# A chunked recurrence with top-k routing on one core: scores and comparisons read PSUM, the one-hot table in six operations, fetched rows turned a step later, VectorE's order changed

## The chip, the cores and the metric

The kernel runs on one core of a Trainium2 chip. The metric is device time in microseconds (us) of one execution; the median of three runs is given. Engines are named as in the profile: PE (TensorE matmuls), DVE (VectorE), ACT (ScalarE), POOL (GpSimd) and SP, whose queue issues nearly all transfers.

## The reference, cut to what matters

Two blocks follow each other. The first is a linear recurrence over 768 tokens for 4 batches and 8 heads of 48 channels, with a decay `w` and a bonus `u`; the second scores each of the 768 rows of a batch, takes the 128 best, and sends those alone through a two-layer network of width 1024.

```
for t:  y[t] = r[t] @ (state + u*k[t] (x) v[t]);  state = w*state + k[t] (x) v[t]
x = y as (batch, 768, 384)
scores = x @ w_gate                      # one number per row
top = the 128 rows of the batch with the highest scores
out = x;  out[top] = x[top] + sigmoid(scores[top]) * (relu(x[top] @ w1) @ w2)
```

## The kernel before, in words

**Tiling.** A unit is 128 tokens of one batch with all 8 heads; there are 24 units, 6 to a batch (NC = 6). The loop over `n` (line 515) does one unit per step. In a step, `inner(n)` (PE) forms the state update and the products of keys and queries in the PSUM tile `rp`; `added(n, 0)` and `added(n, 1)` (DVE, line 264) add the running state and give `g`, and ACT scales `g` by the decay into the next state `z` (line 267, four pieces for each); `masked(n)` (DVE, line 259) puts the products into the matrix `at`; `turn(n+1)` (PE) transposes the next unit's keys and queries into `pk` and `pr`, ACT copies `pk` (line 231), and `turned` (DVE, line 236) scales `pr`; `bonus_sum(n+1)` (DVE, line 208) sums the bonus products that POOL made; POOL scales keys (`scaled`), builds the diagonal of `at` from the sums (`diagonal`, line 212) and makes the next bonus products (`bonus`). Then `outer(n-1, n)` on PE completes the output `y` of unit n-1 and begins that of unit n. Last, `rows_of_x(n-1)` copies `y` from PSUM to the SBUF tile `x` on ACT (line 321) and `finish(n-1)` multiplies `x` by the gate weights on DVE, summing to the scores `sc` (line 326), and stores `x` through SP's queue.

**Routing.** `scores_along(b, j)` has PE turn the 128 scores of unit j into rows of a PSUM tile and ACT copy them to `srow` (line 344). `compare(b, j)` on DVE compares them with the scores of units 0 to j, one operation each (line 351), and once for ties (line 353). After the sixth unit `count` adds up the counts, `rank` gives every row its rank, `match` (DVE, line 378) builds the one-hot table `oh` of 128 ranks by 768 rows in one operation, `pick` turns it into row numbers, `fetch` (POOL) gathers those rows from DRAM by an indirect transfer into `xr`, and `chosen` has PE transpose them (line 411). The network follows in eight parts, four `hidden` (line 431) and four `expert` (line 443); `leave` (DVE, line 451) adds the result and POOL scatters it.

**Order.** Every engine and every queue works in the order in which the code is written; the semaphores follow from the data. `plan(b)` (lines 479 to 494) puts the routing of batch b into later steps, in one of two places: "turn" (before `outer`) or "end" (after `finish`). With n = 6(b+1): unit j is compared at the end of step n-4+j, ranked at the end of step n+2, matched at the turn of n+3, fetched at its end, and `chosen` stands at the end of n+4; the eight parts lie two to a step in steps n+5 to n+8. What is left for the last batches is written out after the loop (lines 553 to 586), the parts of batch 2 that remain filling PE while batch 3 is ranked.

**Buffers.** The PSUM name `m` has two banks, and all of the routing and the network share them. `y` has two. Loads run four units ahead; SP's queue has, step by step, the three loads of unit n+4, a slice of the weights in steps 5 to 11, and the store of unit n-1.

## Time and profile before

| | us |
|---|---|
| median of 3 runs | 198.11 (195.6 to 199.34) |
| profiled execution, its own time | 198.54 |
| its span, first to last instruction | 196.8 |
| PE busy | 159.7 (81%) |
| DVE busy | 126.2 (64%) |
| POOL busy | 114.8 (58%) |
| ACT busy | 79.5 (40%) |
| moved by DMA | 24.52 MB |

The busy times are of the whole span; the loop over the 24 units runs from about 13 to 167.5 us, and what follows is the ranking and the network of the last batch. A step of the loop is read here from the start of its first `g` (line 264) to the start of the next step's. In a trace, idle time carries the engine whose event ended it.

### The profile page before, as it was taken

Reading aid. Unit: us, or ns where it says so; the run is one execution under the profiler, and the core shown is the slowest. Engines: PE = TensorE matmul, PEld = TensorE weight load, DVE = VectorE, ACT = ScalarE, POOL = GpSimd, SP = SyncE. Lnnn points to the kernel's source line nnn. Section 1 sums busy time; section 2 is a strip of 40 time slices with the busy share of each in tenths; the row PEclk is TensorE's granted clock in tenths of the full one; section 3 lists DMA queues with packets and bytes.
Section 4 is the critical chain, followed back from the end, with each engine's and each line's share of the span. In section 5 each row is a group of like instructions: output and inputs, shape, how many; then the busy total and the mean of one; then the engine's idle time right before and its main releaser. Section 6 shows DMA issues by size and latency. Waiting matters only on the chain.

```text
span 196.8 us, 8480 instructions
## 1 busy us (share of the span) xinstructions
PE 159.7 (81%) x3608; PEld 136.5 (69%) x3608; DVE 126.2 (64%) x435; ACT 79.5 (40%) x267; POOL 114.8 (58%) x131
## 2 busy tenths in 40 slices
PE   1579967757569947999999299999997789996980
PEld 1269956556559936999678299997686689855840
DVE  3835788888897784287688967776889734821000
ACT  2135755425635362365554255365245633300200
POOL 4499999795568785538439957755569600022002
PEclk9999999999975795899999759999999769999999
DMA  6999997789896699087357817554312111102001
GB/s 108 198 179 179 199 198 175 150 218 190 209 229 169 124 260 224 3 213 155 74 127 163 201 44 161 127 120 88 83 42 85 43 40 45 43 7 73 0 0 40
DMA packets 81508, 24.52 MB, mean 125 GB/s; under 512 B 76352, under 2 KB 80704, under 8 KB 81472
## 3 DMA queue, kind: packets, MB, share of 16 engines
q1 hardware_dynamic: 79856, 22.03, 51.4%
q0 software_dynamic: 512, 1.57, 2.6%
q10 hardware_dynamic: 1104, 0.40, 1.4%
q8 instruction: 28, 0.46, 1.0%
q14 instruction: 8, 0.07, 0.1%
HBM read 18.48 MB, written 5.51 MB: 122 GB/s over the span
## 4 chain that ended last, share of the span: by engine, by line
PE 38%; DVE 17%; issue 15%; ACT 11%; POOL 9%; DMA 7%; POOLq 1%; DVEq 0%
PE m L431 8%; PE y L298 6%; DMA xr<-out_dram,idx 6%; ACT z L267 6%; DVE scr L326 5%; DVE gt L351 5%; PE pk L221 4%; PE rp L254 4%; PE pr L224 3%; PE rp L246 3%; PE y L310 3%; PE y L289 3%; DVE scr L353 3%; ACT x L321 3%; POOL at L212 2%
## 5 line engine op out<-in xcount | busy, mean ns | idle before, releaser
L267 ACT ACTIVATE z<-g,wp 128x48 f32<-128x48 f32 x176 | 44.5, 323 | 58.8 <-DVE g L264 58.8
L212 POOL TENSOR_TENSOR at<-dia,du 128x512 f32<-128x512 f32 x24 | 26.6, 1109 | 36.1 <-DVE du L208 36.1
L298 PE MATMUL y<-vin,at 64*64 64x48 f32 x768 | 39.5, 232 | 9.0 <-DVE g L264 8.7
L298 PEld LDWEIGHTS y<-vin,at 64*64 64x64 f32 x768 | 33.4, 146 | 14.9 <-DVE g L264 11.3
L326 DVE SCALAR_TENSOR_TENSOR scr<-x,wg 128x384 f32<-128x384 f32 x24 | 22.3, 929 | 24.7 <-ACT x L321 24.6
L310 PE MATMUL y<-z,rh 48*64 48x48 f32 x352 | 28.7, 229 | 0.0
L204 POOL TENSOR_TENSOR rku<-rk,ub 128x384 f32<-128x384 f32 x24 | 25.9, 1080 | 1.9
L202 POOL TENSOR_TENSOR rk<-rpad,kin 128x384 f32<-128x384 f32 x23 | 26.8, 1167 | 0.0
L431 PE MATMUL m<-xt,w 128*128 128x128 f32 x192 | 25.9, 290 | 0.6 <-ACT xt L413 0.6
L431 PEld LDWEIGHTS m<-xt,w 128*128 128x128 f32 x192 | 24.1, 203 | 1.3 <-ACT xt L413 0.8
L351 DVE TENSOR_SCALAR_CACHE_REDUCE gt<-srow,sc 128x128 bf16<-128x128 f32 x84 | 24.0, 336 | 0.7 <-ACT srow L344 0.7
L198 POOL TENSOR_TENSOR kw<-kin,wk 128x384 f32<-128x384 f32 x23 | 23.7, 1031 | 0.1
L264 DVE TENSOR_TENSOR g<-rp,z 128x192 f32<-128x192 f32 x40 | 14.1, 353 | 15.0 <-ACT z L267 8.7
L443 PE MATMUL m<-w,ht 128*128 128x384 f32 x64 | 23.1, 497 | 0.1
L310 PEld LDWEIGHTS y<-z,rh 48*64 48x64 f32 x352 | 20.8, 146 | 0.0
L289 PE MATMUL y<-z,rh 48*64 48x48 f32 x352 | 20.7, 240 | 0.0
L254 PE MATMUL rp<-rh,kh 48*64 48x64 f32 x768 | 19.6, 244 | 1.0 <-issue 0.6
L221 PE MATMUL pk<-ident,kw 128*112 128x128 f32 x92 | 17.6, 322 | 0.8 <-POOL kw L198 0.8
L224 PE MATMUL pr<-ident,rpad 128*112 128x128 f32 x96 | 17.7, 314 | 0.6 <-issue 0.5
L254 PEld LDWEIGHTS rp<-rh,kh 48*64 48x64 f32 x768 | 16.7, 156 | 1.4 <-issue 1.4
L246 PE MATMUL rp<-vin,kw 64*48 64x48 f32 x704 | 16.1, 225 | 1.9 <-POOL kw L198 1.9
L259 DVE COPY_PREDICATED at<-mask,rp 128x512 f32<-128x512 uint32 x24 | 17.4, 723 | 0.0
(86 smaller groups left out, 238.2 us busy)
## 6 DMA issues: line engine op xcount, KB each, us to landing
rpad<-in_r_dram SPq DMA_DIRECT2D x24, 192.0 KB, 5.0
vin<-in_v_dram SPq DMA_DIRECT2D x24, 192.0 KB, 3.2
out_dram<-x SPq DMA_DIRECT2D x24, 192.0 KB, 3.2
kin<-in_k_dram SPq DMA_DIRECT2D x23, 192.0 KB, 4.6
w<-in_moe_w_dram SPq DMA_DIRECT2D x3, 512.0 KB, 5.0
w<-in_moe_w_dram SPq DMA_DIRECT2D x4, 384.0 KB, 4.4
k<-in_k_dram SPq DMA_DIRECT2D x1, 192.0 KB
ub<-in_u_dram ACTq DMA_DIRECT2D x1, 192.0 KB, 4.6
```

Source lines behind the costliest of these rows:

```text
L202: nc.gpsimd.tensor_mul(rk, rpads[n % NIN][:, :, :D], KIN[n])
L204: nc.gpsimd.tensor_mul(RKU[n], rk, ub)
L212: nc.gpsimd.tensor_mul(AT[n], dia[:, None, :].to_broadcast([128, H, C]), DU[n].rearrange("t i p -> t (i p)")[:, :, None].to_broadcast([128 ...
L221: nc.tensor.transpose(pk[:CH, hp, :], two_heads(kws[n % 3] if keys is None else keys, hp), ident)
L254: nc.tensor.matmul(out=rp[ts, i, hp * C : (hp + 1) * C], lhsT=KH[n][rows, hp, ts], rhs=RH[n][rows, hp, ts], start=True, stop=True)
L267: nc.scalar.activation(to[:, hp, :], g[:, hp, :], AF.Copy, scale=wc[:, hp : hp + 1])
L289: nc.tensor.matmul(out=YP[m][ts, 2 * hp + i, :], lhsT=RH[m][rows, hp, ts], rhs=z[rows, hp, :], start=(hp == 0), stop=False, skip_group_che ...
L298: mm = nc.tensor.matmul(out=y[ts, 2 * hp + i, :], lhsT=AT[n][ts, i * NP + hp, :], rhs=VIN[n][ts, 2 * hp + i, :], start=False, stop=False, ...
L310: nc.tensor.matmul(out=y[ts, 2 * hp + c, :], lhsT=RH[n][rows, hp, ts], rhs=z[rows, hp, :], start=False, stop=(hp == NP - 1), skip_group_ch ...
L326: nc.vector.scalar_tensor_tensor(scr, x, 1.0, wg, op0=OP.mult, op1=OP.mult, accum_out=sc[b][:, c : c + 1])
L351: nc.vector.tensor_scalar(GT[b][:, c, j, :], SR[b, j], sc[b][:, c : c + 1], None, op0=OP.is_gt, op1=OP.add, accum_out=counts[b % 2][:, c, ...
L431: nc.tensor.matmul(out=ph[:, f % 4, :], lhsT=w1[:, d, f * 128 : (f + 1) * 128], rhs=XT[b, z][:, d, :], start=(d == 0), stop=(d == KD - 1))
```

## The change

Six edits. `finish` reads `y` in PSUM for the scores, and the copy to `x` on ACT is made to wait for that. `scores_along` leaves the turned scores in PSUM, and `compare` reads them there; ACT's copy to `srow` is gone. `match` uses six operations, one for each unit, each also writing an accumulator that nobody reads (`found`), on a table of 128 columns in place of 768; the offset of each unit goes into a new column of `counts`. `compare` and `count` move from the end of a step to its turn. `chosen` moves from the end of step n+4 to the turn of n+5, and the eight parts move half a step back: one at the end of n+5, two in each of n+6 to n+8, one at the turn of n+9. `bonus_sum(n+1)` moves ahead of `added(n, 1)`.

```diff
--- before.py
+++ after.py
@@ -171,15 +171,19 @@
     ones = const.tile([128, 2], BF16)
     nc.vector.memset(ones[:, 0:1], -1.0)
     nc.vector.memset(ones[:, 1:2], 0.0)
-    counts = [const.tile([128, NC, NC + 1], F32, name=f"counts{i}") for i in range(2)]
+    counts = [const.tile([128, NC, NC + 2], F32, name=f"counts{i}") for i in range(2)]
     for x in counts:
         nc.vector.memset(x, 0.0)
-    slots = const.tile([128, NC, 128], F32)
+    slots = const.tile([128, 128], F32)
+    found = const.tile([128, NC], F32)
     tok = const.tile([128, NU, 2], BF16)
 
     def late_tables():
-        nc.gpsimd.iota(slots, pattern=[[-128, NC], [1, 128]], base=0, channel_multiplier=0,
+        nc.gpsimd.iota(slots, pattern=[[1, 128]], base=0, channel_multiplier=0,
                        allow_small_or_imprecise_dtypes=True)
+        for x in counts:
+            nc.gpsimd.iota(x[:, :, NC + 1], pattern=[[128, NC]], base=0, channel_multiplier=0,
+                           allow_small_or_imprecise_dtypes=True)
         nc.gpsimd.iota(tok[:, :, 0], pattern=[[0, NU]], base=0, channel_multiplier=1,
                        allow_small_or_imprecise_dtypes=True)
         nc.gpsimd.iota(tok[:, :, 1], pattern=[[T, NU]], base=0, channel_multiplier=0,
@@ -316,21 +320,21 @@
 
     stores, moves = {}, {}
 
-    def rows_of_x(n):
-        b, c = divmod(n, NC)
-        return nc.scalar.copy(xa[b][:, c, :], YP[n].rearrange("t h d -> t (h d)"))
-
     def finish(n):
         b, c = divmod(n, NC)
+        y = YP[n].rearrange("t h d -> t (h d)")
         x = xa[b][:, c, :]
-        nc.vector.scalar_tensor_tensor(scr, x, 1.0, wg, op0=OP.mult, op1=OP.mult,
-                                       accum_out=sc[b][:, c : c + 1])
+        score = nc.vector.scalar_tensor_tensor(scr, y, 1.0, wg, op0=OP.mult, op1=OP.mult,
+                                               accum_out=sc[b][:, c : c + 1])
+        left = nc.scalar.copy(x, y)
+        tc.add_manual_dep(left.ins, score.ins.name, wait_for, reason="one reader of y's bank at a time")
         st = nc.sync.dma_start(out=out[b, c * T : (c + 1) * T, :], in_=x)
         for (bb, _), others in moves.items():
             if bb != b:
                 for o in others:
                     tc.declare_no_dep(st.ins, o.ins, reason="rows of another batch")
         stores.setdefault(b, []).append(st)
+        return left
 
 
     SR, GT, QQ, XR, XT, IDX, GA, HT, PH, PE, OH = ({} for _ in range(11))
@@ -339,9 +343,8 @@
 
     def scores_along(b, j):
         p = psum.tile([128, 512], F32, name="m", bufs=2)
-        nc.tensor.transpose(p[:, :128], sc[b][:, j : j + 1].to_broadcast([128, 128]), ident)
-        SR[b, j] = work.tile([128, 128], F32, name="srow", bufs=3)
-        nc.scalar.copy(SR[b, j], p[:, :128])
+        SR[b, j] = p[:, :128]
+        nc.tensor.transpose(SR[b, j], sc[b][:, j : j + 1].to_broadcast([128, 128]), ident)
 
     def compare(b, j):
 
@@ -370,12 +373,13 @@
 
     def match(b, z):
         oh = OH[b, z] = work.tile([128, NC, 128], BF16, name="oh")
+        q = QQ[b]
         if z:
             q = work.tile([128, NC], F32, name="qz")
             nc.vector.tensor_scalar(q, QQ[b], float(-128 * z), None, op0=OP.add)
-        else:
-            q = QQ[b]
-        nc.vector.tensor_tensor(oh, slots, q[:, :, None].to_broadcast([128, NC, 128]), op=OP.is_equal)
+        for c in range(NC):
+            nc.vector.tensor_scalar(oh[:, c, :], slots, q[:, c : c + 1], None, op0=OP.is_equal, op1=OP.add,
+                                    accum_out=found[:, c : c + 1])
 
     def pick(b, z):
         p = psum.tile([128, 512], F32, name="m", bufs=2)
@@ -480,18 +484,18 @@
         n = (b + 1) * NC
         for j in range(NC):
             step(n - NC + j + 2, "turn", scores_along, b, j)
-            step(n - NC + j + 2, "end", compare, b, j)
-        step(n + 1, "end", count, b)
+            step(n - NC + j + 2, "turn", compare, b, j)
+        step(n + 1, "turn", count, b)
         step(n + 2, "end", rank, b)
         for z in range(NST):
             step(n + 3, "turn", match, b, z)
             step(n + 3, "end", pick, b, z)
             step(n + 3, "end", fetch, b, z)
-            step(n + 4, "end", chosen, b, z)
+            step(n + 5, "turn", chosen, b, z)
         parts = [p for z in range(NST) for p in mlp(b, z)]
         per = -(-len(parts) // 8)
         for i, (f, a) in enumerate(parts):
-            step(n + 5 + i // per // 2, ("turn", "end")[i // per % 2], f, *a)
+            step(n + 5 + (i // per + 1) // 2, ("end", "turn")[i // per % 2], f, *a)
 
     for b in range(B):
         plan(b)
@@ -531,11 +535,12 @@
         masked(n)
         if n + 1 < NU:
             pr = turn(n + 1)
+        if n + 1 < NU:
+            bonus_sum(n + 1)
         if c < NC - 1:
             added(n, 1)
         if n + 1 < NU:
             turned(n + 1, pr)
-            bonus_sum(n + 1)
         if n + 2 < NU:
             scaled(n + 2)
         if n + 1 < NU:
@@ -545,8 +550,7 @@
         work_at(n, "turn")
         outer(n - 1 if n else None, n, G[n, 0])
         if n:
-            left = rows_of_x(n - 1)
-            finish(n - 1)
+            left = finish(n - 1)
         work_at(n, "end")
 
 
@@ -565,7 +569,6 @@
     scores_along(last, NC - 2)
     outer(NU - 1, None, left)
     compare(last, NC - 2)
-    rows_of_x(NU - 1)
     finish(NU - 1)
     some(NST)
     scores_along(last, NC - 1)
```

## Rows read from the trace of the kernel before

**Rows 1.** Busy time of each engine by stage, one row per window of time.

```profile
core 0: us, PE busy (x) PEld busy (x) DVE busy (x) ACT busy (x) POOL busy (x), PEclk, DMA share, GB/s
...
21.88:56.79 34.91, 24.40 (x813) 20.98 (x811) 29.45 (x98) 16.96 (x62) 28.95 (x30) 0.99 0.87 194
56.79:69.37 12.58, 12.06 (x296) 11.12 (x296) 9.40 (x27) 6.15 (x22) 8.81 (x9) 0.61 0.72 163
69.37:77.66 8.29, 4.27 (x116) 3.70 (x117) 4.55 (x17) 3.45 (x12) 6.42 (x6) 0.75 1.09 271
77.66:105.91 28.25, 28.25 (x636) 24.27 (x637) 19.88 (x71) 13.98 (x44) 15.06 (x15) 0.95 0.53 117
105.91:114.14 8.23, 4.69 (x145) 4.26 (x144) 7.66 (x17) 2.97 (x11) 7.21 (x9) 0.81 0.76 166
...
120.57:146.72 26.15, 26.15 (x630) 22.16 (x629) 19.80 (x72) 12.57 (x43) 16.21 (x16) 1.00 0.47 105
...
152.81:160.19 7.38, 5.46 (x122) 4.72 (x120) 4.05 (x18) 3.55 (x12) 3.10 (x5) 0.73 0.19 56
...
167.50:196.80 29.30, 21.92 (x142) 16.33 (x142) 6.11 (x30) 3.29 (x8) 3.15 (x5) 0.99 0.08 27
```

**Rows 2.** Chain of work that ended last, step 3: start, length, what.

```profile
29.08 0.97 ACT z L267 x4
30.05 0.15 ACT srow L344
30.20 0.38 ACT x L321
...
30.60 1.06 DVE scr L326 x2
31.67 0.54 DVE gt L351 x4
32.20 0.47 DVE scr L353 x2
```

**Rows 3.** DVE in order of time, step 4: start, length, line, operation.

```profile
32.60 0.35 DVE L264 TENSOR_TENSOR g<-rp,z 128x192 f32<-128x192 f32 x1
32.87 0.72 DVE L259 COPY_PREDICATED at<-mask,rp 128x512 f32<-128x512 uint32 x1
34.02 0.36 DVE L264 TENSOR_TENSOR g<-rp,z 128x192 f32<-128x192 f32 x1 [0.43 <-ACT z L267]
34.30 0.68 DVE L236 TENSOR_TENSOR rh<-pr,tr 112x512 f32<-112x512 f32 x1
34.89 0.54 DVE L208 TENSOR_REDUCE du<-rku 128x8 f32<-128x384 f32 x1
35.98 1.06 DVE L326 SCALAR_TENSOR_TENSOR scr<-x,wg 128x384 f32<-128x384 f32 x1 [0.54 <-ACT x L321]
```

**Rows 4.** Groups by line: busy, mean ns of one, idle before.

```profile
L326 DVE SCALAR_TENSOR_TENSOR scr<-x,wg 128x384 f32<-128x384 f32 x24 | 22.3, 929 | 24.7 <-ACT x L321 24.6
...
L353 DVE SCALAR_TENSOR_TENSOR scr<-srow,sc,earlier 128x128 f32<-128x128 f32 x24 | 12.7, 530 | 0.0
...
L451 DVE SCALAR_TENSOR_TENSOR ot<-m,gate,xr 128x384 f32<-128x384 f32 x4 | 2.4, 612 | 15.8 <-PE m L443 15.8
```

**Rows 5.** DVE in order of time, two operations with POOL busy and POOL idle.

```profile
108.66 3.19 DVE L378 TENSOR_TENSOR oh<-slots,qq 128x768 bf16<-128x768 f32 x1
...
168.48 0.56 DVE L326 SCALAR_TENSOR_TENSOR scr<-x,wg 128x384 f32<-128x384 f32 x1
...
172.26 0.96 DVE L378 TENSOR_TENSOR oh<-slots,qq 128x768 bf16<-128x768 f32 x1
```

**Rows 6.** Chain of work that ended last, fetch and two network parts.

```profile
69.50 5.45 DMA xr<-out_dram,idx
...
89.41 1.53 PE m L431 x12
...
93.51 1.29 PE m L443 x4
```

## The prediction

> **What bounds the kernel now.** I read the busy times by stage first [rows 1]. Three kinds of stage show. In steps 2 to 7 (21.88 to 56.79 us) no engine is full: in 34.91 us DVE is busy 29.45, POOL 28.95, PE 24.40, ACT 16.96. In steps 11 to 14 and 17 to 20, with two network parts each, PE is busy all the time (28.25 of 28.25, 26.15 of 26.15). Step 10 takes 8.29 us and step 22 takes 7.38, with PE busy 4.27 and 5.46 in them. After the loop come 29.30 us.

> What ties the first stage together is in the chain of waits of step 3 [rows 2]: ACT's second set of `z`, the copy to `srow`, the copy to `x`, then on DVE the score, the comparisons, and the next `g`. ACT works in order, so `x` is copied behind `z` and `srow`, and DVE can do nothing between the bonus sum and the score: it stands 0.54 us there, and 0.43 us more between `masked` and the second `g` [rows 3]. All comparisons lie behind the score and ahead of the next `g`. Over the loop DVE waits 24.6 us for the copy to `x` [rows 4].

> DVE's time is partly not its own. The score reads two SBUF tiles and takes 0.56 us where POOL is idle, 0.93 on average and 1.06 in step 4; the one-hot operation takes 0.96 or 3.19 us [rows 3 to 5]. Operations with one input in PSUM (`g`, `rh`) don't vary so [rows 3].

> Step 10 is long for the gathered rows: 5.45 us of its chain are the indirect transfer [rows 6], and PE stands in `chosen` with the next unit behind it. Step 22 is built alike.

> **The change, part by part.**

> **Score and comparisons.** The score needs no copy, so it starts when `y` is done. Its nearest row is `leave`, the same shape with one input in PSUM: 0.61 us [rows 4]; I take 0.65 with its accumulator read. The comparisons move ahead of it, into the time in which PE makes `y`. So DVE's own work sets the step wherever it is the longest: `g` 0.27, `masked` 0.72, `g` 0.28, `rh` 0.59, `du` 0.54 make 2.40 [rows 3] (`du`, moved up, fills the 0.43 us of waiting for `z`); a comparison is 0.27 [rows 2], the tie operation 0.30 (an estimate by the comparison, which has its size; its mean of 0.53 [rows 4] holds the slowing by POOL). With j+1 comparisons that is 3.35 + 0.27(j+1): 3.6 for j = 0 to 5.0 for j = 5.

> Reading PSUM may cost more. [...] The rows give `g`, 192 columns with one input in PSUM, 0.27 to 0.28 from start to start [rows 3] and a comparison of 128 columns in SBUF also 0.27 [rows 2], but `leave` 0.05 more than the lone score [rows 4, 5]. I take no price for the comparisons, as `g` is nearest in size; the other end is 0.05 on the 33 such operations in the steps that DVE bounds, 1.7 us.

> **POOL and PE as floors.** With no operation on two SBUF tiles left on DVE, POOL too should run undisturbed: 16.21 us in four steps [rows 1], 4.05 a step. PE's floor is (28.25 + 26.15)/8 = 6.8 in a step with two parts, and less two parts of 1.41 (the mean of 1.53 and 1.29 [rows 6]) 4.0 without.

> The copy to `x` now follows the score, beside the next `g`: ACT has 16.96 us of work in 34.91 [rows 1], so this hides; were it not hidden it would put its 0.38 [rows 2] on each step. SP's store waits as long, and the loads of the next step stand behind it in that queue; they serve a unit four steps on, which covers it.

> **Steps 2 to 10.** By the largest of the three: steps 2 to 7 take 4.1, 4.1, 4.2, 4.4, 4.7 and 5.1 (with `count`), 26.6 for 34.9. Step 8, with the ranking on PE: 4.4. Step 9 has `match`: six operations of the comparison's form, 6 x 0.27 = 1.6 in place of 0.96 to 3.19, and step 9 is 3.9 + 1.6 = 5.5. Together 9.9 for 12.58. Step 10 without the stall: 4.2 for 8.29; the moved transposes now find rows that had a step to arrive. Saved 15.1.

> **Steps 11 to 23.** The parts now lie one, two, two, two, one. Steps 11 to 14 are 5.9 (one part, and 0.5 for the three transposes, an estimate from twelve matmuls of that width in 1.53 [rows 6]) + 3 x 6.8 = 26.3 for 28.25. Step 15 carries one part, `leave` (0.6), `match` (1.6) and two comparisons (DVE 3.9) with some 0.4 of waiting for the last part: 6.5 for 8.23. Step 16: 4.2 for 6.43 (114.14 to 120.57). Steps 17 to 20: 26.3 for 26.15. Step 21 like 15: 6.5 for 6.09. Step 22: 4.2 for 7.38. Step 23, one part for two and the transposes: 5.9 for 7.31. Saved 9.9.

> **After the loop.** One part more falls here, 1.4 us on PE; the score's start gains the copy's 0.5, and `match` loses 0.6 against its lone 0.96, both beside PE's filling. I take 0.9 more than 29.30; the ends are 0 and 1.4.

> **Transfers.** From 21.88 to 77.66 the DMA engines are busy 0.87 x 34.91 + 0.72 x 12.58 + 1.09 x 8.29 = 48.5 us [rows 1]; I have cut these steps to 40.7. So 7.8 us of transfers must come later. The weights among them are needed only in steps 11 to 14, where the share was 0.53, and a unit's loads run about a step (4.3) ahead of need: I charge 3.5; the ends are 0 and 7.8.

> **The sum.** -15.1 - 9.9 + 0.9 + 3.5 = -20.6. The profiled execution took 198.54, 0.4 over the median of 198.11: 177.9, and I say 178.

> **The rivals.**

> *Transfers bind* (0.13). All 7.8 us show as POOL waiting for keys: 182 to 183. For it: share 0.87 already; against: nothing waits for a load in the middle of the loop now.

> [...]

> *PE's clock stays low* (0.10). [...]

> *Little is gained* (0.08). Something holds steps 2 to 9 at their old length, POOL's chain (28.95 of 34.91) or ACT's order, and only the two stalls for gathered rows (4.1 + 3.2) go, less the tail's 0.9: 192 to 196.

> *Slower* (0.07). The turned scores now keep one of the two `m` banks until the last comparison, 3.0 to 4.3 us into the step, where ACT freed it in 0.15 [rows 2]; the network's sums hold the other in steps 11 to 15, 17 to 21, 23 and after. If PE must wait for that bank ahead of `outer`, `y`, the score and the next `g` all come later. From 1.9 us in each of about 13 such steps it eats the whole 20.6 and the 2% beyond: 203. Against: the next user of a bank mostly stands after `outer`, when the comparisons are done.

> **How the numbers follow.** The forecast has 0.55; its own range is 172 (no transfer stall, tail at its lower end, two parts in 6.4) to 184. The cases from 172 to 190 hold 0.85, so the range is 172 to 190. A time differs from no change here by more than about 2%, so below 194.1 is faster: 0.55 + 0.13 + 0.07 + 0.10 = 0.85; the same 0.08; slower 0.07.

> **What would show it.** In the changed kernel's trace: steps 2 to 4 of 4.0 to 4.4 us; the score at 0.6 to 0.7 us with no wait for ACT before it; comparisons still 0.27 apart; no tie operation over 0.4; POOL's operations near 1.0; no wait of PE for gathered rows in steps 10 and 22; `match` 1.6 us. I am wrong if PE waits on DVE ahead of `outer` or of a part, if POOL or DVE waits for `kin`, or if steps 2 to 7 stay over 5 us.

## The result: 189.7 us for 197.8, and the profile after

The changed kernel takes 189.69 us (median of 4 runs, 185.62 to 192.22), the kernel before 197.82 beside it (195.6 to 199.34): a ratio of 0.947, 95% interval 0.9325 to 0.9615. That is faster, as forecast, and just inside the range of 172 to 190, but the gain is 8 us by the medians and some 10 by the ratio, where 20 were forecast. The profiled execution is the fastest of the four: 185.62 us, its span 183.8, against 198.54 and 196.8 before. The ratio is of the faster executions alone, and the tables below are of one of them: the three slower of the four ran at a mean granted clock of 0.917 to 0.933, where it ran at 0.948, and took 3.7 to 6.6 us more.

First the page of the changed kernel: busy time of each engine with its share and number of instructions, the queue of instruction packets (packets, MB, share), and the chain's shares.

```profile
span 183.8 us, 8493 instructions
...
PE 155.6 (85%) x3608; PEld 131.9 (72%) x3608; DVE 114.9 (62%) x479; ACT 75.4 (41%) x243; POOL 106.3 (58%) x133
...
q8 instruction: 28, 0.46, 1.1%
...
PE 55%; issue 21%; DVE 9%; POOL 8%; ACT 3%; DMA 1%; POOLq 1%; DVEq 0%
```

DVE lost 11.3 us of work and POOL 8.5 without an operation of POOL's loop being changed. PE's share of the chain rose from 38 to 55%, and that of "issue", time in which an engine waits for nothing that the profile names, from 15 to 21%. Most of this "issue" lies at the start and in the tail; but idle time of PE of this kind, called unnamed in what follows, is 11.57 us in all, where it was 1.36 before.

The same stages as in [rows 1], windows set to the steps of the changed kernel (steps 2 to 7; 8 and 9; 10; 11 to 14; 15; 16; 17 to 20; 21; 22; the tail):

```profile
core 0: us, PE busy (x) PEld busy (x) DVE busy (x) ACT busy (x) POOL busy (x), PEclk, DMA share, GB/s
21.04:53.53 32.49, 23.80 (x807) 21.18 (x806) 24.74 (x97) 16.38 (x56) 26.68 (x32) 0.92 0.90 192
53.53:66.15 12.62, 12.44 (x300) 11.21 (x300) 9.11 (x39) 5.39 (x20) 6.99 (x8) 0.65 0.83 198
66.15:70.63 4.48, 3.62 (x123) 3.25 (x122) 4.03 (x17) 3.14 (x11) 4.12 (x4) 1.00 0.78 224
70.63:97.22 26.59, 26.00 (x635) 22.49 (x634) 17.41 (x69) 13.68 (x42) 17.79 (x18) 1.00 0.76 173
97.22:105.42 8.20, 6.72 (x149) 5.10 (x148) 5.96 (x28) 2.93 (x10) 5.97 (x8) 1.00 0.53 123
105.42:109.48 4.06, 4.06 (x128) 3.82 (x128) 3.94 (x14) 2.44 (x9) 2.57 (x4) 1.00 0.85 168
109.48:135.92 26.44, 25.83 (x631) 22.19 (x629) 17.35 (x71) 12.50 (x41) 17.41 (x18) 1.00 0.50 112
135.92:143.99 8.07, 6.93 (x151) 5.26 (x150) 5.96 (x27) 2.93 (x10) 5.10 (x7) 1.00 0.15 52
143.99:148.79 4.80, 4.80 (x121) 4.40 (x120) 4.03 (x15) 2.79 (x10) 1.07 (x2) 0.64 0.15 44
...
154.40:183.80 29.40, 22.98 (x153) 17.52 (x152) 6.00 (x33) 3.62 (x8) 3.15 (x5) 0.97 0.08 28
```

| steps | before | forecast | after |
|---|---|---|---|
| 2 to 7 | 34.91 | 26.6 | 32.49 |
| 8, 9 | 12.58 | 9.9 | 12.62 |
| 10 | 8.29 | 4.2 | 4.48 |
| 11 to 14 | 28.25 | 26.3 | 26.59 |
| 15 | 8.23 | 6.5 | 8.20 |
| 16 | 6.43 | 4.2 | 4.06 |
| 17 to 20 | 26.15 | 26.3 | 26.44 |
| 21 | 6.09 | 6.5 | 8.07 |
| 22 | 7.38 | 4.2 | 4.80 |
| 23 | 7.31 | 5.9 | 5.61 |
| tail | 29.30 | 30.2 | 29.40 |

Nearly all of the missing gain lies in two places. Steps 2 to 9 took 8.6 us more than their terms, against 3.5 charged for transfers; and of these steps, 2 to 6 are near the forecast (4.22, 4.86, 4.45, 4.50, 4.61, each from the start of its first `g` to the next), while step 7 takes 9.85 and step 8 7.08. Steps 15 and 21 took 3.3 more than theirs.

**Where the parts did what they should.** DVE in order of time, steps 3 and 4 of the changed kernel (start, length, line, operation, idle before it), against [rows 3]:

```profile
31.24 0.55 DVE L212 TENSOR_REDUCE du<-rku 128x8 f32<-128x384 f32 x1 [0.18 <-POOL rku L208]
31.71 0.35 DVE L268 TENSOR_TENSOR g<-rp,z 128x192 f32<-128x192 f32 x1
31.97 0.68 DVE L240 TENSOR_TENSOR rh<-pr,tr 112x512 f32<-112x512 f32 x1
32.57 0.34 DVE L354 TENSOR_SCALAR_CACHE_REDUCE gt<-m,sc 128x128 bf16<-128x128 f32 x1
32.83 0.08 DVE L354 DVE_READ_ACCUMULATOR gt<-m,sc 128x1 f32 x1
32.83 0.35 DVE L354 TENSOR_SCALAR_CACHE_REDUCE gt<-m,sc 128x128 bf16<-128x128 f32 x1
...
33.84 0.56 DVE L327 SCALAR_TENSOR_TENSOR scr<-y,wg 128x384 f32<-128x384 f32 x1
34.33 0.08 DVE L327 DVE_READ_ACCUMULATOR scr<-y,wg 128x1 f32 x1
34.51 0.36 DVE L268 TENSOR_TENSOR g<-rp,z 128x192 f32<-128x192 f32 x1
```

The bonus sum fills the wait for `z`, the comparisons run where DVE stood idle for the copy, 0.26 to 0.28 us apart, and the score takes 0.56 with no wait ahead of it. Groups by line (busy, mean ns of one, idle before), of DVE and POOL:

```profile
L354 DVE TENSOR_SCALAR_CACHE_REDUCE gt<-m,sc 128x128 bf16<-128x128 f32 x84 | 24.6, 347 | 4.4 <-PE m L347 4.3
L268 DVE TENSOR_TENSOR g<-rp,z 128x192 f32<-128x192 f32 x40 | 14.2, 356 | 19.2 <-PE rp L258 17.5 <-ACT z L271 1.4
L327 DVE SCALAR_TENSOR_TENSOR scr<-y,wg 128x384 f32<-128x384 f32 x24 | 13.3, 556 | 5.9 <-PE y L314 4.2
L356 DVE SCALAR_TENSOR_TENSOR scr<-m,sc,earlier 128x128 f32<-128x128 f32 x24 | 8.4, 348 | 0.0
L206 POOL TENSOR_TENSOR rk<-rpad,kin 128x384 f32<-128x384 f32 x23 | 23.1, 1003 | 0.0
```

The score fell from 929 to 556 ns on average and the tie operation from 530 to 348 [rows 4]; `rk` on POOL fell from 1167 to 1003 ns, with the same operands as before. DVE's idle time has moved from ACT's copy (24.6 us) to PE's `rp` (17.5).

**Where it didn't.** PE's restarts after the two longest idle stretches of the changed kernel, both in step 7 as cut here, then what the DMA engines did in that step (busy tenths in 40 slices), and the engines' busy times in steps 7 and 8:

```profile
46.83 0.43 PE L228 MATMUL pr<-ident,rpad 128*112 128x128 f32 x2 [2.67 <-issue]
52.88 0.48 PE L258 MATMUL rp<-rh,kh 48*64 48x64 f32 x4 [2.33 <-issue]
```

```profile
DMA  9999999999412954999588999999999999610906
...
DMA packets 6457, 1.98 MB, mean 201 GB/s; under 512 B 6175, under 2 KB 6315, under 8 KB 6455
...
q8 instruction: 2, 0.03, 1.3%
...
w<-in_moe_w_dram SPq DMA_DIRECT2D x2, 512.0 KB, 5.6
```

```profile
43.62:53.47 9.85, 4.84 (x137) 4.13 (x136) 5.05 (x24) 3.30 (x11) 4.97 (x6) 0.75 0.99 201
53.47:60.55 7.08, 7.08 (x154) 6.52 (x154) 3.69 (x13) 2.93 (x10) 3.96 (x4) 0.50 0.80 195
```

Both gaps lie in the middle of a row of like matmuls (the second half of the transposes, the last four products), with nothing named that PE waits for. What comes just before each restart is a packet on the queue marked "instruction". Its 28 packets, 0.46 MB together, are 16 KB each; if they hold PE's 3608 matmuls and 3608 loads, that makes by my estimate some 258 instructions to a packet, and a step of the first stage has 807/6 = 135 matmuls and as many loads, 269: about one packet a step. From the transfer records, for every unnamed idle stretch of PE over 0.5 us (the last column is the place of the restarting instruction in the row of all that the trace records of PE: matmuls, loads and semaphore waits):

```
kernel   PE restarts  after idle  last packet moved   restart after its end   instruction
before      53.93       0.60      51.44 to 52.58            1.34                2242
after       27.94       1.02      25.61 to 26.63            1.31                 962
after       32.37       0.98      29.70 to 31.02            1.35                1218
after       37.06       0.88      34.45 to 35.50            1.56                1474
after       41.15       0.69      38.62 to 39.77            1.38                1730
after       46.83       2.67      44.43 to 45.48            1.35                1986
after       52.88       2.33      50.43 to 51.48            1.40                2242
after       69.52       0.86      66.71 to 68.06            1.46                3009
```

In this table the restart always comes 1.31 to 1.56 us behind a packet's end, and the first six of the changed kernel are exactly 256 instructions apart; the seventh is three times 256 further on, less one (now and then a record is missing). The 68 unnamed gaps of over 0.5 us in the loop, in all 14 profiles here, lie at this count, to within that one, and that of the kernel before at the same 2242. I read this as PE having used up a block of 256 instructions and standing until the next was there; what a packet holds no record shows. The two long gaps can be added up: PE ran through the block begun at 41.15 in 3.01 us; the next packet began to move 3.28 us after that start, took 1.05, and PE restarted 1.35 behind it, 5.68 in all, and 5.68 less 3.01 is the gap of 2.67. And the granted clock falls after the first of the two: it is 0.50 from 48.63 to 62.28, in all of step 8 too, in which PE is busy 7.08 of 7.08 us. Gap and clock together make the 7.7 us by which steps 7 and 8 (16.93) exceed the 9.2 that they take where the gaps are short (below).

### The profile page after: what moved, and what is told of

Same layout as the page of the kernel before. It is cut to its first block, busy times and chain, and to the rows that moved or that the text cites. A ratio compares the mean times of both kernels' runs of the same rounds, so it can differ in the third digit from the quotient of the medians.

```text
span 183.8 us, 8493 instructions
## 1 busy us (share of the span) xinstructions
PE 155.6 (85%) x3608; PEld 131.9 (72%) x3608; DVE 114.9 (62%) x479; ACT 75.4 (41%) x243; POOL 106.3 (58%) x133
## 3 DMA queue, kind: packets, MB, share of 16 engines
q0 software_dynamic: 512, 1.57, 2.8%
## 4 chain that ended last, share of the span: by engine, by line
PE 55%; issue 21%; DVE 9%; POOL 8%; ACT 3%; DMA 1%; POOLq 1%; DVEq 0%
PE y L302 10%; PE rp L258 8%; PE rp L250 6%; PE m L435 6%; PE pk L225 5%; PE m L447 5%; PE y L314 4%; PE pr L228 4%; PE y L293 4%; DVE oh L381 3%; ACT z L271 2%; POOL rku L208 2%; POOL rk L206 2%; POOL kw L202 2%; PE m L347 2%
## 5 line engine op out<-in xcount | busy, mean ns | idle before, releaser
L216 POOL TENSOR_TENSOR at<-dia,du 128x512 f32<-128x512 f32 x24 | 25.0, 1042 | 33.8 <-DVE du L212 33.8
L302 PE MATMUL y<-vin,at 64*64 64x48 f32 x768 | 38.7, 228 | 3.0 <-issue 2.9
L329 ACT COPY x<-y 128x384 f32<-128x384 f32 x24 | 11.5, 479 | 46.5 <-DVE scr L327 43.3
L354 DVE TENSOR_SCALAR_CACHE_REDUCE gt<-m,sc 128x128 bf16<-128x128 f32 x84 | 24.6, 347 | 4.4 <-PE m L347 4.3
L268 DVE TENSOR_TENSOR g<-rp,z 128x192 f32<-128x192 f32 x40 | 14.2, 356 | 19.2 <-PE rp L258 17.5
L435 PE MATMUL m<-xt,w 128*128 128x128 f32 x192 | 24.5, 280 | 1.1 <-ACT ht L438 0.6
L208 POOL TENSOR_TENSOR rku<-rk,ub 128x384 f32<-128x384 f32 x24 | 24.0, 1000 | 1.9
L258 PE MATMUL rp<-rh,kh 48*64 48x64 f32 x768 | 20.2, 234 | 4.7 <-issue 4.3
L435 PEld LDWEIGHTS m<-xt,w 128*128 128x128 f32 x192 | 22.4, 192 | 2.0 <-ACT ht L438 0.8
L202 POOL TENSOR_TENSOR kw<-kin,wk 128x384 f32<-128x384 f32 x23 | 23.1, 1004 | 0.1
L206 POOL TENSOR_TENSOR rk<-rpad,kin 128x384 f32<-128x384 f32 x23 | 23.1, 1003 | 0.0
L258 PEld LDWEIGHTS rp<-rh,kh 48*64 48x64 f32 x768 | 16.6, 145 | 5.9 <-issue 5.8
L228 PE MATMUL pr<-ident,rpad 128*112 128x128 f32 x96 | 16.7, 301 | 2.7 <-issue 2.7
L240 DVE TENSOR_TENSOR rh<-pr,tr 112x512 f32<-112x512 f32 x24 | 16.4, 682 | 1.8 <-PE pr L228 1.8
```

What stands on the lines that cost most here:

```text
L202: nc.gpsimd.tensor_mul(kws[n % 3][:, :, :D], KIN[n], wk)
L206: nc.gpsimd.tensor_mul(rk, rpads[n % NIN][:, :, :D], KIN[n])
L208: nc.gpsimd.tensor_mul(RKU[n], rk, ub)
L216: nc.gpsimd.tensor_mul(AT[n], dia[:, None, :].to_broadcast([128, H, C]), DU[n].rearrange("t i p -> t (i p)")[:, :, None].to_broadcast([128 ...
L258: nc.tensor.matmul(out=rp[ts, i, hp * C : (hp + 1) * C], lhsT=KH[n][rows, hp, ts], rhs=RH[n][rows, hp, ts], start=True, stop=True)
L302: mm = nc.tensor.matmul(out=y[ts, 2 * hp + i, :], lhsT=AT[n][ts, i * NP + hp, :], rhs=VIN[n][ts, 2 * hp + i, :], start=False, stop=False, ...
```

## The experiments

Four theories were set against each other: that PE's blocks of instructions come late behind data (called F in what follows, or the block theory), that the gaps belong to fixed places of the program and are there whatever is moved, that one part of the change bears most of the gain or costs some of it, and, for steps 15 and 21, several on their own. The kernels ran in three groups, each on a chip of its own with the kernel before beside them (medians 198.07, 197.2 and 197.72). Times are compared by their ratio to that; the changed kernel itself ran again on the first of these chips alone.

**Repetition and later weights (first chip).** `r_after` is the changed kernel again.

> The changed kernel again, as the base for the others of this call. Theory F (PE runs out of instructions: its blocks of 16 KB, 256 instructions, come late behind data transfers): idle time of PE that no data explains in the middle of groups, about 5 us in steps 6 and 7 as in its first profile, each ending 1.0 to 1.3 us after an instruction block has been moved; 186 to 192 us. Rival S (PE is held by semaphores at a fixed place of the program): the same idle times at the same two places, lines 228 and 258 of step 7, to within 0.3 us.

Measured: 185.57 us (184.02 to 192.75, 5 runs), 0.9455 [0.914, 0.977]. The gaps are there again in steps 7 and 8 (2.40 and 1.04 us), at the same two places, and one of 2.10 in step 10.

`e1_weights_late` loads the first weights by columns in steps 7 to 10 and the second in 11 to 13:

```diff
-        if NC - 1 <= n < NC - 1 + KD:
-            d = n - NC + 1
-            nc.sync.dma_start(out=w1[:, d, :], in_=moe_w1[d * 128 : (d + 1) * 128, :])
+        if NC + 1 <= n < NC + 5:
+            f = slice((n - NC - 1) * F // 4, (n - NC) * F // 4)
+            nc.sync.dma_start(out=w1[:, :, f], in_=moe_w1.rearrange("(kd p) f -> p kd f", p=128)[:, :, f])
...
```

> The network's weights are loaded in steps 7 to 13 (w1 in four slices by columns in steps 7 to 10, w2 in 11 to 13) in place of 5 to 11; all else as in the changed kernel. Theory F: the two long idle times of PE in step 7 (2.7 and 2.3 us) go, since they follow the traffic; steps 6 and 7 take 4.5 to 5.2 us each, step 8 keeps the full clock and takes under 5; 4 to 7 us off the whole. Rival S: idle times of 2 us or more stay at lines 228 and 258 of step 7, and the time is as before this edit, within 1 us. Rival D (data arrives late): POOL waits for kin or rpad in steps 5 to 8 of the changed kernel, and no longer here.

Measured: 189.41 us (184.82 to 191.31), 0.970 [0.932, 1.008]: no gain in time is shown. Its steps 7, 8, 15 and 16 (columns as above):

```profile
43.10:48.36 5.26, 3.37 (x134) 2.98 (x134) 4.96 (x25) 2.95 (x11) 4.76 (x6) 1.00 0.72 150
48.36:54.81 6.45, 4.64 (x154) 4.14 (x153) 3.56 (x13) 3.29 (x11) 4.31 (x5) 0.94 0.73 184
91.93:100.26 8.33, 6.98 (x148) 5.27 (x147) 5.96 (x27) 2.93 (x10) 6.10 (x8) 0.89 0.51 120
100.26:106.65 6.39, 6.39 (x122) 5.94 (x122) 4.13 (x15) 2.93 (x10) 3.99 (x5) 0.50 0.59 121
```

Step 7 fell from 9.85 to 5.26 us, with gaps of 0.76 and 1.14 us for 2.67 and 2.33; a gap of 1.80 came in step 8, where this kernel moves weights. Steps 2 to 9 together took 39.38 us for 45.11. The places are those of the count of 256 in every kernel; what changed here with the traffic is how long PE stood there, and this speaks against gaps that are there whatever is moved. But the clock fell to 0.50 in step 16, where the changed kernel's profile had 1.00, and the profile's span came to 183.0, no less than 183.8.

**The parts of VectorE's edit (first chip).** `e2_copy_first` copies `y` to SBUF first and scores from there; `e3_compare_end` has the comparisons behind the score again:

```diff
-        score = nc.vector.scalar_tensor_tensor(scr, y, 1.0, wg, ...)
         left = nc.scalar.copy(x, y)
-        tc.add_manual_dep(left.ins, score.ins.name, wait_for, ...)
+        nc.vector.scalar_tensor_tensor(scr, x, 1.0, wg, ...)
```

```diff
-            step(n - NC + j + 2, "turn", compare, b, j)
-        step(n + 1, "turn", count, b)
+            step(n - NC + j + 2, "scored", compare, b, j)
+        step(n + 1, "scored", count, b)
...
         if n:
             left = finish(n - 1)
+        work_at(n, "scored")
```

> Undoes one edit of the change: ACT copies y to x first and the score reads x in SBUF. All else as changed. The prediction's theory (score and copy on the chain): each step that DVE or PE's y bounds grows by the copy, 0.4 to 0.5 us, and the score goes back to 0.6 to 1.0 us beside POOL: 24 x 0.6 to 0.9 = 14 to 20 us at most, 6 to 12 where the steps with two network parts hide it. Theory F: the steps 2 to 7 are paced by the instruction blocks (4.2 to 4.8 us each), so slack of 0.3 us a step takes up part of it: 2 to 6 us slower than the changed kernel.

> Undoes one edit: the comparisons and the count stand after the score again (still reading PSUM). All else as changed. The prediction's theory: in each step without network parts the comparisons (0.54 to 1.9 us) come back between the score and the next g: steps 2 to 10, 15, 16, 21, 22 grow by 0.5 to 1.9 us, 8 to 13 us slower than the changed kernel in all. Theory F alone (blocks pace the steps, DVE has slack): under 4 us.

Measured: 188.34 us, 0.955 [0.918, 0.992], and 189.66, 0.964 [0.929, 0.999]. Neither differs from the repetition (0.9455) by more than the intervals; the 6 to 12 and 8 to 13 us that were expected from the prediction's theory did not show. The traces show both edits where they were made: scored from SBUF, the score takes 690 ns on average for 556; with the comparisons behind it, it waits 24.6 us in all for `y`, time that the comparisons filled (4.2 after). But steps 2 to 6 together take 22.87 and 24.22 us for 22.64: 0.2 and 1.6 us for either edit alone.

**All of VectorE's edit undone, and all of the plan's (second chip).** `e7_chain_back` is the changed kernel with both edits above, and with `srow` copied by ACT and the bonus sum behind the second `g` as before, so that only `match`, `chosen` and the moved parts remain of the change. `e4_old_plan` undoes these moves alone:

```diff
-            step(n + 5, "turn", chosen, b, z)
+            step(n + 4, "end", chosen, b, z)
...
-            step(n + 5 + (i // per + 1) // 2, ("end", "turn")[i // per % 2], f, *a)
+            step(n + 5 + i // per // 2, ("turn", "end")[i // per % 2], f, *a)
```

> Puts the whole chain of before back: copy to x first and the score from SBUF, turned scores copied to SBUF by ACT, comparisons and count after the score, bonus sum after the second g. What stays of the change: one-hot in six operations, fetched rows turned a step later, the network's parts half a step later. The prediction's theory: steps 2 to 9 return to 5.3 to 7 us; some 8 to 12 us slower than the changed kernel, 4 to 10 faster than before. Theory F (instruction blocks pace PE in steps 2 to 8 of the changed kernel): the same direction, but PE's unexplained idle time falls from 11 us to under 4, as each step gives the blocks more time, so only 5 to 9 us are lost.

> Undoes one edit: fetched rows are turned at the end of step n+4 again and the parts lie two to a step from n+5. All else as changed. The prediction's theory: PE stands for the indirect transfer at the end of steps 10, 16 and 22, 3 to 5 us in 10 and 22; 5 to 9 us slower than the changed kernel. Rival: the loss is hidden because POOL and DVE, now ahead, issue the fetch earlier; under 3 us. If the short idle times of PE at line 258 in steps 15 and 21 (1.2 us in each) come from POOL's two indirect transfers lying side by side, they go here, where the scatter is a step earlier; if they belong to the place behind the one-hot product, they stay.

Measured: `e7_chain_back` 195.61 us (10 runs), 0.9958 [0.986, 1.006]; `e4_old_plan` 190.46, 0.966 [0.950, 0.982]. With VectorE's edit gone nothing is left of the gain that can be measured, where 4 to 10 us were expected to be left: steps 2 to 6 take 27.89 us (28.23 before, 22.64 after), and what `chosen` saves in steps 10 and 11 (11.08 for 16.19) is given back in 13 and 19 (9.36 and 9.34 for 7.53 and 7.54). With `chosen` in its old place PE waits for the fetched rows again: its transposes in step 10 before, in `e4_old_plan`, and after.

```profile
74.99 0.90 PE L411 MATMUL m<-ident,xr 128*128 128x128 f32 x3 [3.62 <-DMA xr<-out_dram,idx]
71.25 0.86 PE L415 MATMUL m<-ident,xr 128*128 128x128 f32 x3 [1.57 <-DMA xr<-out_dram,idx]
71.28 0.49 PE L415 MATMUL m<-ident,xr 128*128 128x128 f32 x3
```

Steps 10 and 11 take 7.69 and 8.54 us there, 16.23 for 9.91, but this is not the wait alone: the granted clock is 0.72 and 0.75 in them, and in the repetition, with `chosen` late, they took 14.14 us, with the gap of 2.10 and the clock at 0.50 for 6.8 us. In the whole time 5 to 9 us more than the changed kernel were expected; the ratios of 0.966 and 0.947 are 4 us apart, and their intervals overlap. And PE's unnamed idle time in steps 2 to 9 is 1.81 us in `e7_chain_back`, in steps of 5 us and more, where it is 8.57 after: with the longer steps PE stands less, though the same weights are moved beside them.

**More traffic, and a tidied kernel (second chip).** `e5_traffic` loads 512 KB more in each of steps 16 to 19, into tiles that nobody reads. `e9_tidy` spreads the first weights over twelve transfers of 128 KB in steps 4 to 9 and the second over steps 10 to 13, puts `match` ahead of the result's addition, and moves the gates, which use an `m` bank, to the first `expert` part:

```diff
+        if 2 * NC + 4 <= n < 2 * NC + 8:
+            nc.sync.dma_start(out=idle[n - 2 * NC - 4], in_=moe_w1[:128, :])
```

```diff
+        for i in range(2 * (n - NC + 2), 2 * (n - NC + 3)):
+            if 0 <= i < 4 * KD:
+                f, d = slice(i // KD * F // 4, (i // KD + 1) * F // 4), i % KD
+                nc.sync.dma_start(out=w1[:, d, f], in_=moe_w1[d * 128 : (d + 1) * 128, f])
...
-            step(n + 3, "turn", match, b, z)
+            step(n + 3, "first", match, b, z)
```

> The changed kernel with four more loads of 512 KB, one in each of steps 16 to 19, into tiles that nobody reads; no computation is changed. Theory F: the quiet steps 16 to 19, which show no unexplained idle time of PE, get it: one to three pieces of 0.5 to 2.5 us, each ending 1.0 to 1.4 us after an instruction block was moved; 1 to 5 us in all. Rival S (fixed places of the program): none there, and the pieces in steps 3 to 8 as before.

> Three edits on the changed kernel: weights in smaller pieces and spread (w1 in twelve pieces of 128 KB over steps 4 to 9, w2 in four over 10 to 13); match ahead of leave; the gates product moved from the last hidden part to the first expert part, so that PE no longer waits for an m bank ahead of the turned scores. Theory F with the two small waits (0.6 us in steps 13 and 19, 0.5 in 15 and 21): the pieces of idle time in step 7 shrink from 5 us to under 2.5, and 2 us come from the rest: 181 to 186 us. Rival S: only the 2 us, 184 to 189.

Measured: `e5_traffic` 179.9 us (2 runs), 0.918 [0.902, 0.933], less and not more than the changed kernel; `e9_tidy` 176.4 (174.59 to 178.12, 4 runs), 0.894 [0.879, 0.910]. In step 17 there is a gap that the changed kernel doesn't have, of 1.01 us, and the step takes 6.60 us for 5.22. That the extra loads made it isn't shown: `e9_tidy`, on the same chip and without them, has one of 1.24 us at the same place. In steps 16, 18 and 19, with a load each, no unnamed gap stands, against what F expected. And steps 15 and 21, before and after the loads, took 6.00 us each, where the changed kernel took 8.20 and 8.07. The same in `e9_tidy` (6.05 and 6.04). That had to be settled.

**The weights left out, and the halves of the two (third chip).** `e12_no_weights` loads 16 columns of each slice of the weights and sets the rest once ahead of the loop, so that the network works on other weights; `e11_small` is `e5_traffic` with 8 KB for 512 in each extra load; `e10_spread` has the spread weights of `e9_tidy` alone and `e13_tidy_only` its two moves.

```diff
+    nc.vector.memset(w1, 0.01)
+    nc.vector.memset(w2, 0.01)
...
-            nc.sync.dma_start(out=w1[:, d, :], in_=moe_w1[d * 128 : (d + 1) * 128, :])
+            nc.sync.dma_start(out=w1[:, d, :16], in_=moe_w1[d * 128 : (d + 1) * 128, :16])
```

> The kernel after with 16 columns of each weight slice loaded instead of the whole slice (steps 5 to 11), the rest of both tables set once by VectorE ahead of the loop: the network works on other weights, and 3 MB less are moved. Block theory (PE's 16 KB blocks of instructions come late because the weights fill the queues): the long idle stretches of PE in steps 7 and 8 (2.67 and 2.33 us after, 2.40 and 1.04 in its repetition) shrink to under 1.0 us each, steps 7 and 8 take 5.0 and 4.6 us instead of 9.85 and 7.08, and the granted clock doesn't fall there; the time is 6 to 8 us lower than that of the kernel after in the same profile, some 178 us. Rival (the stretches belong to fixed places of the program, whatever else is moved): steps 7 and 8 stay at 9 and 7 us, and the time at 185 to 190. In steps 15 and 21 neither predicts a change (8.2 us); only the layout theory does not exclude one.

Measured: 184.43 us (182.81 to 188.5, 4 runs), 0.940 [0.918, 0.963]; steps 7 and 8 of its profile, then step 16, and PE's restarts at the two places:

```profile
46.14:51.15 5.01, 3.76 (x134) 3.28 (x135) 4.87 (x25) 2.82 (x10) 4.50 (x6) 1.00 0.92 196
51.15:55.33 4.18, 4.18 (x155) 3.84 (x154) 3.56 (x14) 3.26 (x11) 3.15 (x4) 1.00 0.66 149
100.61:106.03 5.42, 5.42 (x122) 5.13 (x122) 4.03 (x16) 2.93 (x10) 3.92 (x5) 0.58 0.70 139
```

```profile
46.14 0.43 PE L230 MATMUL pr<-ident,rpad 128*112 128x128 f32 x2 [0.58 <-issue]
50.60 0.33 PE L260 MATMUL rp<-rh,kh 48*64 48x64 f32 x4 [1.14 <-issue]
```

Steps 7 and 8 take 9.19 us for 16.93, and the clock doesn't fall there: as the block theory had it, to 0.4 us. The gaps stand at the same two places of the program, and last 0.58 and 1.14 us for 2.67 and 2.33 with 3 MB less moved. The packets that ended them began to move, by an estimate, 1.6 and 2.0 us after PE had begun the block before (at 42.10 and 46.14), if from there to the restart it was 2.40 and 2.45 us as in the changed kernel; there it was 3.28 and 3.60. Steps 2 to 9 take 36.75 us, where 45.11 were measured with the weights and 36.5 forecast. The median came out 6 us over the expected 178, and 0.940 is not apart from the 0.947 of the changed kernel: in the time of the whole the gain isn't shown. Two things make up for it in the profiled execution: setting the tables put the loop back by 3.07 us (its first `g` starts at 15.53 for 12.46), and the clock fell in steps 16 and 17, which took 12.05 us for 9.28. From the first `g` to that of step 9 the kernel takes 39.80 us for 48.09 after, with 1185 matmuls for 1184.

> The kernel after with the first weights in twelve pieces of 128 KB, two a step in steps 4 to 9, and the second in four pieces in steps 10 to 13; no other edit. Block theory: steps 7 and 8 take 7.3 and 5.7 us as in e9_tidy (13.0 instead of 16.9), so 3 to 4 us less than the kernel after, and 13 and 19 stay at 7.8: 181 to 185 us, depending on steps 15 and 21. If the short stretches there come from the order of match, pick and the addition, they stay, at 8.2 us (185); if from where instructions lie, they may go, and the time is 179 to 181. Rival (fixed places): steps 7 and 8 unchanged, 185 to 190 us.

> The two moves of e9_tidy without its spread weights: the one-hot operations go ahead of the result's addition in steps 9, 15 and 21, and the gates (one m bank) to the first expert part. By the order on the engines: steps 13 and 19 take 7.1 us instead of 7.8 (the wait of 0.6 us for the m bank is gone), steps 15 and 21 take 6.1 instead of 8.2, because pick's wait for the one-hot table goes and the short stretches with it; steps 7 and 8 stay at 9 to 10 and 7 us. Together 1.4 + 4.2 less than the kernel after: 180 us (178 to 182). If the short stretches in steps 15 and 21 come from where instructions lie and not from that wait, they may stay: 8.2 us there, 13 and 19 at 7.1, and 184 to 188 us in all.

Measured: `e10_spread` 183.34 us (181.1 to 186.51), 0.926 [0.909, 0.942], within what was expected: steps 7 and 8 take 10.85 us for 16.93, with a gap of 1.85 us there, and another of 1.60 in step 4 makes that 5.86 us for 4.45. `e13_tidy_only` 187.91 (186.29 to 189.36), 0.955 [0.942, 0.968]: steps 13 and 19 take 7.14 us for 7.84, so the gates' bank was what PE waited for there, but steps 15 and 21 take 8.37 and 8.32. The order of `match` is not their cause.

> The same instructions as e5_traffic, transfer for transfer, but each of the four extra transfers of steps 16 to 19 moves 8 KB (128 x 16 numbers) instead of 512 KB: what is left of e5 is the layout of the program and of the buffers, and what is gone is its traffic. Layout theory (e5 was faster because its instructions or buffers lie elsewhere): about 180 us (179 to 181.5), steps 15 and 21 take 6.0 us, without the three idle stretches of some 0.4 us at L258, and no stretch of 1.0 us in step 17. Traffic theory (the bytes themselves made e5 faster): like the kernel after, 184 to 190 us, steps 15 and 21 at 8.1 to 8.3 us with the three stretches. The block theory (PE waits for a block of instructions behind data) says nothing against either, but by it the 1.0 us of idle PE that e5 had in step 17 goes.

Measured: 186.99 us (184.12 to 190.09, 4 runs, against 197.72), steps 15 and 21 at 8.21 and 8.08: as the traffic theory expected, and the layout theory falls. No unnamed gap is left in step 17. PE in step 15 of `e11_small` and then of `e5_traffic`, which have the same instructions:

```profile
101.26 0.57 PE L251 MATMUL rp<-vin,kw 64*48 64x48 f32 x32
101.66 0.67 PE L259 MATMUL rp<-rh,kh 48*64 48x64 f32 x13
102.75 0.39 PE L259 MATMUL rp<-rh,kh 48*64 48x64 f32 x8 [0.43 <-issue]
103.56 0.33 PE L259 MATMUL rp<-rh,kh 48*64 48x64 f32 x4 [0.42 <-issue]
104.30 0.38 PE L259 MATMUL rp<-rh,kh 48*64 48x64 f32 x7 [0.41 <-issue]
```

```profile
100.24 0.57 PE L251 MATMUL rp<-vin,kw 64*48 64x48 f32 x32
100.64 0.76 PE L259 MATMUL rp<-rh,kh 48*64 48x64 f32 x32
```

Yet the traffic theory can't be right as it stood: the extra loads begin only in step 16, and `e9_tidy`, `e7_chain_back` and `e4_old_plan` have no such stretches in step 15 either, without extra loads. What orders the runs is the chip. All four profiles of the second chip are free of the short stretches; all eight of the first and third have two or three of them in each of steps 15 and 21, among them both halves of `e9_tidy` and the twin of `e5_traffic`. The changed kernel itself was not run on the second chip, and why one chip differs is **open**: these stretches of 0.16 to 0.46 us don't follow the instruction packets as the gaps above do (in the changed kernel's own profile the five restarts at line 258 stand 0.25 to 4.47 us behind one, at instructions 4624, 4642, 4652, 6438 and 6468, none of them at the count of 256). One rival is untested: they come only in the two steps in which POOL issues the scatter and the next fetch one behind the other, and not in step 9, which has the fetch alone; `e4_old_plan`, which moves the scatter a step ahead, ran on the chip that shows none. They cost some 2 us in each of the two steps, 8.2 for 6.0, and often the clock after them: in the repetition step 16 took 6.39 us at 0.50, in the changed kernel's profile 4.06 at 1.00. So 176.4 us for `e9_tidy` is a measured time, the best here, but 4 us and more of its lead over `e10_spread` and `e13_tidy_only` may be the chip's.

## Why the prediction was right, and where it was not

**The range: right by 0.3 us, and by luck.** 189.69 lies within 172 to 190 because the range took in the rival of the clock (189 by an estimate of mine, a chance of 0.10). The forecast of 178 and its own range to 184 were missed. In the profiled execution the miss is 7.7 us, and the tables tell where; the rest of the 11.7 lies between that execution and the median. (From the median of 198.11 the sum gives 177.5, not 177.9; that decides nothing.)

**Score and comparisons: right.** Steps 2 to 6 came to 22.64 us for 21.5 forecast (4.1, 4.1, 4.2, 4.4, 4.7), and undoing this part as a whole took the gain away (`e7_chain_back`); the score or the comparisons put back singly cost nothing clear of the noise.

**PSUM reads: the value taken was right.** A comparison from PSUM stands 0.27 us behind the last, as it did from SBUF [rows 2], and the mean is 347 ns for 336. The score took 0.56, not 0.65. No run shows the price of PSUM reads that the 0.07 in the sum of the chances stands for; what they show is these 11 ns on a comparison.

**POOL: right.** `rk` fell from 1167 to 1003 ns once DVE had no operation on two SBUF tiles in the loop, and rose to 1018 (and `kw` from 1004 to 1114) in `e2_copy_first`, which brings one back, with the score at 690 ns for 556. In `e7_chain_back`, with the score and the tie operation reading SBUF alone again, these take 911 and 613 ns (556 and 348 after) and `rk` 1153: in these runs both sides took longer beside each other. Why they do the traces don't show.

**`chosen` a step later: right.** Step 10 takes 4.48 us (4.2 forecast), with no wait for the rows; in `e4_old_plan` PE waits 1.57 us for them there, of the 3.62 before. What it is worth in the whole time is not shown.

**Transfers: the step that failed.** I charged 3.5 us, with ends of 0 and 7.8, in the form of POOL waiting for keys. POOL never waited for `kin`. What came late, as I read the restarts, was PE's own instructions: PE stood up to 2.67 us at places 256 instructions apart, and went on 1.31 to 1.56 us behind a 16 KB packet of the instruction queue, which no row of the profile's idle times names. Steps 2 to 9 took 8.6 us over their terms, more than the upper end; without the weights (`e12_no_weights`) they took 36.75 us, 0.25 over their terms, and 7.7 of what is given back lies in steps 7 and 8. The trace of before did show it: three gaps of 0.31 to 0.60 us, each restart 1.31 to 1.46 us behind a packet, in steps of over 5 us. I read PE's idle time there as slack.

**PE's clock: a rival of 0.10 that came about in part,** and not as I had it. Its 189 is an estimate: the eleven steps without parts at 5.4 us each, half-way from the 4.5 of my terms to the 6.3 that steps 8 and 9 took at a clock of 0.61 before [rows 1]. No run shows a clock that is low throughout these steps: in the changed kernel it fell to 0.50 for 13.65 us, over the second half of step 7, step 8 and the first third of 9, from 1.80 us behind the gap of 2.67, and for 3.4 in step 22. In all nine profiles with a gap of 2 us or more it fell during the gap or within 1.8 us of its end (the four transposes to `pk` take 0.65 us at 1.00 and 1.10 at 0.50); where the gaps were short (`e12_no_weights`) it stayed at 1.00 from 19.59 to 60.55 us. A long gap does not always stand ahead of it: in the kernel before it fell at 56.38, and no unnamed gap was over 0.60.

**Steps 15 and 21: 1.7 and 1.6 us too low.** A wait of 0.4 for the last part was foreseen; the short stretches were not, and their cause is open.

**The `m` banks: the "slower" rival's mechanism exists, at about a twentieth of its price.** PE waited 0.59 us for a bank ahead of the turned scores in step 13, and moving the gates took 0.70 off each of steps 13 and 19. Together 1.4 us; to decide it needed 1.9 us in 13 steps.

**Match and tail: right.** `match` takes 1.6 us; the tail 29.40, which did not grow by the 0.9 that I added.

## What to carry to other kernels

When steps get shorter, ask what each engine needs per step that isn't data: here PE, with 269 instructions in a step, saw about one 16 KB packet of the instruction queue per step, and in step 7, with two loads of 512 KB beside it, stood 2.67 and 2.33 us with no wait named, where it stood 0.58 and 1.14 with 8 KB for each of them. Look for "issue" gaps in the middle of a row of equal instructions, and compare their ends with the instruction queue; then spread the loads: in `e10_spread` steps 2 to 9 took 40.1 us for 45.1, in `e1_weights_late` 39.4, though what this is worth in the whole time is not clear of the noise here. And take a chip's own gaps into account before giving a difference of 2% to an edit.
